# Linear attention with a norm, then an ELU MLP: the first batch worked in chunks of two heads

## The chip, the cores and the metric

The kernel runs on one core of a Trainium2 chip. Its engines work in parallel, each through its own list of instructions: PE (TensorE, matrix multiplies into PSUM, the accumulation memory), ACT (ScalarE, functions of one operand), DVE (VectorE, elementwise work), POOL (GpSimd, elementwise work, and here the issuer of most loads) and SP (SyncE, which issues other transfers). An engine takes its instructions strictly in order, so an instruction that waits holds up all behind it. Transfers between the chip's main memory and SBUF, the memory that the engines work on, are moved by 16 DMA engines that all queues share.

The metric is the device time of one execution in microseconds (us), as the median of several runs.

## The reference

```python
# q, k, v: (8, 8, 576, 64) float32; g_norm: (64,)
kv = np.einsum('bhsd,bhse->bhde', k, v)
out = np.einsum('bhsd,bhde->bhse', q, kv)
rms = np.sqrt(np.mean(out * out, axis=-1, keepdims=True) + 1e-06)
attn = out / rms * g_norm
# heads side by side: x is (8 * 576, 512)
x = attn.transpose(0, 2, 1, 3).reshape(B * S, H * D)
# w_in: (512, 2048), w_out: (2048, 512)
h = x @ w_in
g = np.where(h > 0.0, h, np.exp(np.minimum(h, 0.0)) - 1.0)
return g @ w_out
```

For each of 8 batches and 8 heads a 64x64 matrix K^T V is formed, Q is multiplied by it, and each row of 64 is divided by its root mean square and scaled by g_norm. The 4608 rows of 512 then go through two matrix multiplies with an ELU between them.

## The kernel before

**Tiles.** The 4608 rows of x are worked in nine tiles T of 512 rows. Matmuls take bf16 operands. For each tile the first multiply (mm1, line 378) makes h in eight pairs of 128x512 blocks, i = 0 to 7; each pair goes through the ELU (Exp on ACT, line 350; two operations on DVE, lines 358 and 362) into gT; the second multiply (mm2, line 399) takes gT in 16 blocks f against w_out, which arrives in four loads of four blocks each.

**Chunks.** A batch's q, k and v lie in SBUF as four chunks of two heads each, chunk m on 128 partitions with 9x64 columns. In the code a chunk has a number c = 2l + u. K^T V of a pair u = 0 (chunks 0 and 2) or u = 1 (chunks 1 and 3) is worked at once: `kv_mm` (line 152) issues 9 x 2 x 2 small matmuls. xT, the operand of mm1, has four parts c = 0 to 3, one for each chunk; mm1 needs all four to finish a block.

**The steps of a pair in tile 0**, which is batch 0 but for its last 64 rows of 576: q is turned by PE (`turned_q`, line 502) and copied to qT (`q_t_out`); K^T V is formed in PSUM and copied to kv_sb (`kv_out`, one half on DVE and one on ACT); the product y is made on PE (`y_mm`); then the class `Turned` squares y on ACT (line 229), PE takes the mean with a matrix of 1/64 (`mean_mm`, line 199), ACT makes Ln and Exp(-0.5 x) of it (`inv_t`, lines 208 and 209), and DVE multiplies y by that and by g (`scale_t`, line 212) into one part of xT.

**The head, in the order of the code** (lines 464 to 611). The order of all instructions on an engine is that of the code; it is written out by hand.

- SP loads batch 0 in fp32 by pairs of chunks: q, k, v of pair 0 (288 KB as bf16, 576 KB as fp32, each), then q and k of pair 1 and, into the buffer of the first q once this is cast, v of pair 1.
- DVE, ACT and, for pair 1, POOL cast these to bf16 (`first_cast`, columns low = 5 of 9 and high = 4 of 9).
- POOL issues all loads of the weights and of the later batches. These cast on the way from fp32 to bf16. Its list is: cast of q; w_in for blocks 0 to 4, rows 0 and 2; cast of k; the same, rows 1 and 3; cast of v; w_in for the other blocks in three loads; w_out(0); the first halves of q, k, v of batch 1; w_out(1); the second halves; w_out(2) and (3); batch 2; batch 3.
- PE fills its gaps with matmuls on zeros (`idle`, line 498): 9 at the start, then 10, 2, 1, 7 and 2, in all 31, into banks that are not in use.
- The first blocks of mm1 of tile 0 (`early`, line 578) are made part by part: h0, h1 and one half of h2 with parts c = 0 and 2, then c = 1, then c = 3, then the other half of h2 with all four. After these PE goes on with mm1 for i = 3 to 7 (line 611), and then with mm2 of tile 0 between the steps of batch 1 (lines 627 to 656).

PSUM has eight banks here under the tags A and B (pairs of banks), m and x (two single banks each). A new tile under a tag waits until the older one in the same bank has been read.

Of the kernel before, what the change touches and what calls it, by code (L numbers as in the profile page):

```python
# [16 lines left out]
def kernel(  # L17
# [90 lines left out]
    def copy_on(eng, out_, in_):  # L108
        if eng is nc.scalar:
            nc.scalar.copy(out_, in_)  # L110
# [40 lines left out]
    def kv_mm(b, kv_ps, u):
        for j in range(RK):
            for s in range(2):
                rows = slice(s * 64, s * 64 + 64)
                for l in range(2):
                    nc.tensor.matmul(  # L156
                        kv_ps[s][l * 64 : l * 64 + 64, u * 64 : u * 64 + 64],
                        lhsT=bf["k", b][rows, 2 * l + u, j, :],
                        rhs=bf["v", b][rows, 2 * l + u, j, :],
                        start=(j == 0),  # L160
                        stop=(j == RK - 1),
                    )
# [18 lines left out]
    def y_mm(T, u, ps, ns=slice(0, 8)):  # L181

        n = ns.start
        while n < ns.stop:
            b, j = slot_of(T, n)
            m = min(ns.stop - n, RK - j)
            for l in range(2):
                for s in range(2):
                    nc.tensor.matmul(  # L189
                        ps[l][s * 64 : s * 64 + 64, n * 64 : (n + m) * 64],  # L190
                        lhsT=kv_of(b, l, u, s),
                        rhs=qT[b][l * 64 : l * 64 + 64, s, u, j : j + m, :],
                        start=True,
                        stop=True,
                    )
            n += m

    def mean_mm(sq, ps):
        nc.tensor.matmul(ps, lhsT=ones, rhs=sq, start=True, stop=True)  # L199
# [7 lines left out]
    def inv_t(r, ps):  # L207
        nc.scalar.activation(r, ps, AF.Ln, bias=eps_col)  # L208
        nc.scalar.activation(r, r, AF.Exp, scale=-0.5)  # L209
# [251 lines left out]

    first = {}

    def first_load(name, u, st):
        first[name, u] = st
        load(st, name, 0, slice(u, 4, 2), nc.sync)

    def first_tile(name):  # L470
        return stage.tile([P, 2, RK, D], FP32, name=f"first_{name}", tag=f"first_{name}")

    def first_cast(name, u, eng, js):
        copy_on(eng, bf[name, 0][:, u::2, js, :], first[name, u][:, :, js, :])
# [14 lines left out]
    nc.vector.memset(zeros, 0.0)
    nc.vector.memset(eps_col, 1e-6)  # L490
    nc.vector.memset(one, 1.0)  # L491
    nc.vector.memset(ones, 0.0)
    for l in range(2):
        nc.vector.memset(ones[l * 64 : l * 64 + 64, l * 64 : l * 64 + 64], 1.0 / D)

    idle_ps = pair("B", "idle_ps")

    def idle(n, ps=idle_ps[:, 0, :]):
        for _ in range(n):
            nc.tensor.matmul(ps, lhsT=zeros[:, 0:P], rhs=zeros, start=True, stop=True)  # L500

    def turned_q(b, u, tag):

        ps = as_bf16(single(tag, "qt_ps"))
        q_t_mm(b, u, range(8), ps)
        return ps

    qT_tile(0)
    x_tile(0)
    g_ps = pair("A", "g_ps")  # L510
    idle(9)
    nc.tensor.transpose(g_ps[:, 0, 0:1], g_row.rearrange("o l e -> o (l e)"), one)
    nc.vector.tensor_copy(out=g_col, in_=g_ps[:, 0, 0:1])
    first_cast("q", 0, V, low)
    first_cast("q", 0, A, high)
    first_load("v", 1, first_tile("q"))
    ps = turned_q(0, 0, "m")
    idle(10)
    q_t_out(0, 0, V, ps, slice(0, 8))
    first_cast("k", 0, A, high)  # L520
    first_cast("k", 0, V, low)
    first_cast("v", 0, V, low)
    first_cast("v", 0, A, high)
    kv_ps = [single("x", "kv_ps") for _ in range(2)]
    kv_mm(0, kv_ps, 0)
    idle(2)
    kv_out(0, kv_ps, 0, (V, A))
    first_cast("q", 1, V, low)
    first_cast("q", 1, Q, high)
    load_w_in(slice(0, 5), slice(0, KC, 2))  # L530
    first_cast("k", 1, Q, high)
    load_w_in(slice(0, 5), slice(1, KC, 2))
    first_cast("v", 1, Q, high)
# [16 lines left out]
    y_ps = pair("A", "y_ps")  # L550
    n0.product([y_ps[:, l, :] for l in range(2)])
    for l in range(2):
        n0.square(l)
    ps = turned_q(0, 1, "m")
    q_t_out(0, 1, V, ps, slice(0, 8))
    first_cast("k", 1, V, low)
    first_cast("v", 1, V, low)
    idle(1)
    for l in range(2):
        n0.sums(l, single("x", "mean"))  # L560
        n0.inv(l)
    idle(7)
    kv_ps = pair("B", "kv_ps")
    kv_ps = [kv_ps[:, s, :] for s in range(2)]
    kv_mm(0, kv_ps, 1)
    kv_out(0, kv_ps, 1, (V, A))
    n0.scale(0)
    n0.scale(1)
    y_ps = [single("m", "y_ps") for _ in range(2)]
    idle(2, y_ps[0])  # L570
    n1.product(y_ps)
    for l in range(2):
        n1.square(l)
    g_tile(0)
    h0, h1 = pair("B", "h_ps"), pair("A", "h_ps")
    mean, h2 = single("x", "mean"), [single("x", "h_ps"), None]

    def early(h, i, a, cs):

        for c in cs:  # L580
            nc.tensor.matmul(  # L581
                h[a] if isinstance(h, list) else h[:, a, :],
                lhsT=w_in_sb[:, c, (2 * i + a) * P : (2 * i + a) * P + P],
                rhs=xT[0][:, c, :],
                start=(c == 0),
                stop=(c == KC - 1),
            )

    for a in range(2):
        early(h0, 0, a, (0,))  # L590
    n1.sums(0, mean)
    n1.inv(0)
    n1.scale(0)
    for a in range(2):
        early(h0, 0, a, (2,))
    for a in range(2):
        early(h1, 1, a, (0, 2))
    n1.sums(1, mean)
    n1.inv(1)
    n1.scale(1)  # L600
    early(h2, 2, 0, (0, 2))
# [181 lines left out]
```

## Time and profile before

| | |
|---|---|
| median of 7 runs | 294.97 us (294.12 to 295.32) |
| the profiled execution | 295.08 us |
| its span, first to last instruction | 293.3 us |
| mean granted TensorE clock in the span | 0.997 |
| first square of batch 0 on ACT | 10.19 us after the span's start |
| first matmul of `early` | 16.37 us |
| first matmul of mm1 for i = 3 | 22.86 us |
| POOL's first load (w_in) issued | 10.64 us |
| w_out(2) wanted by PE until | 42.47 us |

In the timeline each line holds the start, the duration, the engine, the line of the code, the operation, what it writes and reads, the shapes, the count of instructions merged into it and, in brackets, how long the engine sat idle before it and what ended that. In the table of stages each engine has its busy time and, in brackets, its count; then come the granted clock, the busy share of the DMA engines and what they moved in GB/s. A matmul of 128x512 is listed with 379 ns of busy time, but they overlap: eight start within 1.73 us, so one each 0.216 us.

### The profile page before, as it was taken

Reading aid. Unit: us, or ns where it says so; the run is one execution under the profiler, and the core shown is the slowest. Engines: PE = TensorE matmul, PEld = TensorE weight load, DVE = VectorE, ACT = ScalarE, POOL = GpSimd, SP = SyncE. Lnnn points to the kernel's source line nnn. Section 1 sums busy time; section 2 is a strip of 40 time slices with the busy share of each in tenths; the row PEclk is TensorE's granted clock in tenths of the full one; section 3 lists DMA queues with packets and bytes.
Section 4 is the critical chain, followed back from the end, with each engine's and each line's share of the span. In section 5 each row is a group of like instructions: output and inputs, shape, how many; then the busy total and the mean of one; then the engine's idle time right before and its main releaser. Section 6 shows DMA issues by size and latency. Waiting matters only on the chain.

```text
span 293.3 us, 5198 instructions
## 1 busy us (share of the span) xinstructions
PE 282.5 (96%) x2152; PEld 130.1 (44%) x2152; DVE 167.2 (57%) x221; ACT 142.1 (48%) x210; POOL 44.8 (15%) x79
## 2 busy tenths in 40 slices
PE   7979989998999999999999999999999999999994
PEld 3434434443444444444444444444444444444443
DVE  2538823478259855874577557755775677444600
ACT  3658445768555525542554255425542554244310
POOL 0663432213300002403300330000000000000000
PEclk9999999999999999999999999999999999999998
DMA  7999999996921089968943896362331214020222
GB/s 261 269 171 206 208 204 208 310 233 192 187 43 36 18 132 247 213 88 182 252 112 70 162 260 131 63 128 72 38 82 26 72 37 105 2 74 0 72 72 75
DMA packets 46236, 38.95 MB, mean 133 GB/s; under 512 B 26372, under 2 KB 38916, under 8 KB 46212
## 3 DMA queue, kind: packets, MB, share of 16 engines
q0 software_dynamic: 14144, 19.53, 34.2%
q1 hardware_dynamic: 31664, 18.55, 28.7%
q10 hardware_dynamic: 404, 0.53, 0.5%
q8 instruction: 17, 0.28, 0.4%
q14 instruction: 7, 0.06, 0.1%
HBM read 36.70 MB, written 9.44 MB: 157 GB/s over the span
## 4 chain that ended last, share of the span: by engine, by line
PE 79%; DMA 12%; DVE 3%; POOL 2%; ACT 2%; SPq 0%; issue 0%; DVEq 0%
PE o_ps L399 38%; PE h_ps L378 37%; DMA w_out_sb<-in_moe_w_out_dram 9%; DMA st_q<-in_q_dram 3%; DVE gT L362 2%; PE at L250 2%; POOL w_in_sb L116 1%; PE at L156 1%; PE o_ps L436 1%; ACT elu_e L350 1%; DVE elu_e L358 1%; DVE xT L212 0%; SPq L90 0%; PE qt_ps L174 0%; POOL q_bf L112 0%
## 5 line engine op out<-in xcount | busy, mean ns | idle before, releaser
L399 PE MATMUL o_ps<-w_out_sb,gT 128*128 128x512 bf16 x560 | 130.9, 379 | 1.5 <-DMA w_out_sb<-in_moe_w_out_dram 0.8
L378 PE MATMUL h_ps<-xT,w_in_sb 128*128 128x512 bf16 x552 | 128.9, 379 | 0.9 <-DVE gT L362 0.6
L350 ACT ACTIVATE elu_e<-h_ps 128x1024 bf16<-128x1024 f32 (+1 forms) x77 | 73.9, 972 | 92.1 <-PE h_ps L378 89.2
L362 DVE TENSOR_TENSOR gT<-elu_e,h_ps 128x1024 bf16<-128x1024 bf16 (+1 forms) x73 | 85.6, 1177 | 7.3
L399 PEld LDWEIGHTS <-gT 128*128 128x128 bf16 x560 | 54.4, 98 | 67.7 <-issue 3.3
L378 PEld LDWEIGHTS <-w_in_sb 128*128 128x128 bf16 x552 | 52.4, 98 | 62.6 <-issue 2.0
L358 DVE TENSOR_SCALAR elu_e<-elu_e 128x1024 bf16<-128x1024 bf16 x72 | 31.8, 441 | 68.4 <-ACT elu_e L350 68.2
L415 ACT COPY o_sb<-o_ps 128x512 f32<-128x512 f32 x32 | 18.5, 588 | 18.8 <-PE o_ps L399 18.7
L103 POOL CAST q_bf<-st_q 128x384 bf16<-128x384 f32 x30 | 14.2, 523 | 28.0 <-DMA st_q<-in_q_dram 28.0
L212 DVE SCALAR_TENSOR_TENSOR xT<-y_ps,g_col,rT 128x512 bf16<-128x512 f32 x12 | 8.9, 748 | 16.0 <-ACT rT L209 16.0
L283 DVE TENSOR_REDUCE ss<-sq 128x16 f32<-128x1024 bf16 x12 | 14.6, 1219 | 4.6 <-ACT sq L277 4.6
L299 DVE TENSOR_TENSOR xs<-at,ss 128x1024 bf16<-128x1024 f32 x12 | 14.6, 1217 | 0.0
L277 ACT ACTIVATE sq<-at 128x1024 bf16<-128x1024 f32 x12 | 12.3, 1028 | 1.0 <-PE at L250 1.0
L339 POOL COPY gate<-qT 1x32 bf16<-1x32 bf16 x4 | 0.8, 201 | 73.6 <-DMA qT<-q_bf 73.6
L229 ACT ACTIVATE sq<-y_ps 128x512 bf16<-128x512 f32 x12 | 6.5, 595 | 7.7 <-PE y_ps L189 7.7
L500 PE MATMUL idle_ps<-zeros 128*128 128x512 bf16 x29 | 9.0, 456 | 1.2 <-DVE one L491 1.2
L208 ACT ACTIVATE rT<-mean,eps_col 128x512 f32<-128x512 f32 x12 | 8.2, 683 | 3.0 <-PE mean L199 2.8
L156 PEld LDWEIGHTS <-k_bf 64*64 64x64 bf16 x576 | 5.7, 107 | 5.1 <-issue 4.2
L581 PE MATMUL h_ps<-xT,w_in_sb 128*128 128x512 bf16 x24 | 6.0, 379 | 1.9 <-DMA w_in_sb<-in_moe_w_in_dram 1.3
L209 ACT ACTIVATE rT<-rT 128x512 f32<-128x512 f32 x12 | 7.6, 630 | 0.4
L90 POOL DMA_DIRECT2D k_bf<-in_k_dram x9 | 6.6, 738 | 5.3 <-DMA w_in_sb<-in_moe_w_in_dram 1.9
L90 POOL DMA_DIRECT2D v_bf<-in_v_dram x9 | 6.8, 752 | 4.3 <-DMA w_out_sb<-in_moe_w_out_dram 1.8
(59 smaller groups left out, 97.5 us busy)
## 6 DMA issues: line engine op xcount, KB each, us to landing
out_dram<-o_sb SPq DMA_DIRECT2D x24, 256.0 KB, 4.1
st_q<-in_q_dram POOLq DMA_DIRECT2D x5, 1152.0 KB, 7.4
k_bf<-in_k_dram POOLq DMA_DIRECT2D x5, 576.0 KB, 9.4
v_bf<-in_v_dram POOLq DMA_DIRECT2D x5, 576.0 KB, 13.5
out_dram<-o_sb SPq DMA_DIRECT2D x19, 128.0 KB, 2.6
w_out_sb<-in_moe_w_out_dram POOLq DMA_DIRECT2D x4, 512.0 KB, 13.9
q_bf<-in_q_dram POOLq DMA_DIRECT2D x4, 288.0 KB, 14.0
k_bf<-in_k_dram POOLq DMA_DIRECT2D x4, 288.0 KB, 14.2
```

What stands on the lines that cost most here:

```text
L90: eng.dma_start(out=dst.rearrange("p m j d -> p m (j d)"), in_=in_[:, ms, :])
L103: nc.gpsimd.tensor_copy(out=bf["q", b][:, u, js], in_=raw[b][:, u::2, js, :].rearrange("p l j d -> p j l d"),)
L277: nc.scalar.activation(sq, st["se", h], AF.Square)
L283: nc.vector.reduce_sum(out=ss, in_=st.pop(("sq", h)).rearrange("p l (m e) -> p (l m) e", e=D), axis=AX.X,)
L299: nc.vector.tensor_tensor(out=st["xs"][:, 2 * h : 2 * h + 2, :].rearrange("p i (l m e) -> p l i m e", l=2, e=D), in0=se_ps.rearrange("p l ...
L350: nc.scalar.activation(e[:, lo:hi, :], h, AF.Exp)
L358: nc.vector.tensor_scalar(out=e, in0=e, scalar1=1.0, scalar2=1.0, op0=ALU.min, op1=ALU.subtract)
L362: nc.vector.tensor_tensor(out=gT[T][:, 2 * i + lo : 2 * i + hi, :], in0=e[:, lo:hi, :], in1=h, op=ALU.add if relu else ALU.max,)
L378: nc.tensor.matmul((ps[a] if isinstance(ps, list) else ps[:, a, :])[:, cols], lhsT=w_in_sb[:, c, f * P : f * P + P], rhs=xT[T][:, c, cols] ...
L399: nc.tensor.matmul(o_ps[T, j], lhsT=gT[T][:, f, j * P : j * P + P], rhs=w_out_sb[:, f, :], start=(f == 0), stop=(f == FC - 1),)
L415: nc.scalar.copy(o_sb[T, half][:, j % 2, :], o_ps[T, j])
L500: nc.tensor.matmul(ps, lhsT=zeros[:, 0:P], rhs=zeros, start=True, stop=True)
```

## The change

Tile 0's part of batch 0 is worked chunk by chunk, in the order 0, 2, 1, 3, where it was worked in two pairs.

- **Loads.** SP loads three pieces in fp32: q of chunks 0 and 2, k of chunk 0, v of chunk 0. All other pieces of batch 0 are loads on POOL's queue that cast on the way, straight into the bf16 tiles. POOL's list is: k and v of chunk 2; q of chunks 1 and 3; k and v of chunk 1; w_in for blocks 0 to 4, row 0; k and v of chunk 3; the same blocks of w_in, rows 2, 1, 3, in a load each; and from there the loads of before in their order. POOL's casts of batch 0 go, and DVE's and ACT's casts of pair 1.
- **K^T V.** `kv_mm` and `y_mm` take the halves l to work on as an argument. Each chunk has 18 matmuls and one copy of 64x128 on DVE in place of 36 matmuls and two copies of 128x64 for a pair.
- **Norm.** Square, mean, Ln, Exp and scale are issued for each chunk by itself. For chunks 1 and 3 Exp and scale are in two halves of 256 columns (`chunk_norm`). ACT's order is: square, Ln, Exp of chunk 0; of chunk 2; square, Ln, two Exps of chunk 1; of chunk 3. DVE's order is: copies of K^T V of chunks 0 and 2, the copy of qT of pair 1, scale 0, K^T V of chunk 1, scale 2, both halves of scale 1, K^T V of chunk 3, both halves of scale 3.
- **PE.** 13 matmuls on zeros (8 and 5) where there were 31, all before K^T V of chunk 0. The `early` matmuls are spread between the steps of chunks 1 and 3, and taken part by part in the order 0, 2, 1, 3.

The core of the diff:

```diff
-    def kv_mm(b, kv_ps, u):
+    def kv_mm(b, kv_ps, u, ls=range(2)):
...
-                for l in range(2):
+                for l in ls:
...
     for name in "qkv":
         bf[name, 0] = qkvp.tile([P, 4, RK, D], BF16, name=f"{name}_bf", tag=name)
-        first_load(name, 0, first_tile(name))
-    more = stage.tile([P, 4, RK, D], FP32, name="st_q", tag="q")
-    for name, half in (("q", 0), ("k", 2)):
-        first_load(name, 1, more[:, half : half + 2])
+    first = {"q": first_load("q", (0, 2)), "k": first_load("k", (0,)), "v": first_load("v", (0,))}
...
+    def chunk_load(name, cs):
+        ms = slice(cs[0], cs[-1] + 1, 2)
+        load(bf[name, 0][:, ms], name, 0, ms)
+    chunk_load("k", (2,))
+    chunk_load("v", (2,))
+    chunk_load("q", (1, 3))
+    chunk_load("k", (1,))
+    chunk_load("v", (1,))
+    load_w_in(slice(0, 5), slice(0, 1))
+    chunk_load("k", (3,))
+    chunk_load("v", (3,))
+    for c in (2, 1, 3):
+        load_w_in(slice(0, 5), slice(c, c + 1))
...
+    def chunk_kv(kv_ps, c):
+        kv_mm(0, [kv_ps[:, s, :] for s in range(2)], c % 2, (c // 2,))
+    def chunk_kv_out(kv_ps, c, eng):
+        rows, cols = slice(c // 2 * 64, c // 2 * 64 + 64), slice(c % 2 * 64, c % 2 * 64 + 64)
+        copy_on(eng, kv_sb[rows, 0, c % 2], kv_ps[rows, :, cols])
+    def chunk_y(c, tag):
+        y_ps[c] = single(tag, "y_ps")
+        y_mm(0, c % 2, {c // 2: y_ps[c]}, (c // 2,))
+    def chunk_square(c):
+        sq0[c] = attp.tile([P, G], BF16, name="sq", tag="sq")
+        nc.scalar.activation(sq0[c], y_ps[c], AF.Square)
+    def chunk_inv(c, mean):
+        r0[c] = outp.tile([P, G], FP32, name="rT", tag="o")
+        inv_t(r0[c], mean)
+    def chunk_scale(c):
+        scale_t(0, y_ps[c], r0[c], c)
+    def chunk_norm(c, mean):
+        r0[c] = outp.tile([P, G], FP32, name="rT", tag="o")
+        nc.scalar.activation(r0[c], mean, AF.Ln, bias=eps_col)
+        for n in range(2):
+            cols = slice(n * 256, n * 256 + 256)
+            nc.scalar.activation(r0[c][:, cols], r0[c][:, cols], AF.Exp, scale=-0.5)
+            scale_t(0, y_ps[c][:, cols], r0[c][:, cols], c, cols)
...
+    idle(8, kv_ps[:, 0, :])
+    first_cast("q", (0, 2), V, low)
+    first_cast("q", (0, 2), A, high)
+    ps = turned_q(0, 0, "m")
+    idle(5, kv_ps[:, 0, :])
+    q_t_out(0, 0, V, ps, slice(0, 8))
...
+    chunk_kv(kv_ps, 0)
+    chunk_kv_out(kv_ps, 0, V)
+    chunk_y(0, "x")
+    chunk_square(0)
+    chunk_kv(kv_ps, 2)
+    chunk_kv_out(kv_ps, 2, V)
+    mean = pair("A", "mean")
+    mean_mm(sq0[0], mean[:, 0, :])
+    chunk_inv(0, mean[:, 0, :])
+    chunk_y(2, "x")
+    chunk_square(2)
+    ps = turned_q(0, 1, "m")
+    q_t_out(0, 1, V, ps, slice(0, 8))
+    mean_mm(sq0[2], mean[:, 1, :])
+    chunk_inv(2, mean[:, 1, :])
+    chunk_scale(0)
+    kv_ps = pair("B", "kv_ps")
+    chunk_kv(kv_ps, 1)
+    chunk_kv_out(kv_ps, 1, V)
+    chunk_scale(2)
+    chunk_y(1, "m")
+    chunk_square(1)
...
+    early(h0, 0, 0, (0,))
+    early(h0, 0, 1, (0,))
+    mean_mm(sq0[1], mean)
+    chunk_norm(1, mean)
+    early(h2, 2, 0, (0,))
+    chunk_kv(kv_ps, 3)
+    chunk_kv_out(kv_ps, 3, V)
+    chunk_y(3, "m")
+    chunk_square(3)
+    early(h1, 1, 0, (0,))
+    early(h1, 1, 1, (0,))
+    early(h0, 0, 0, (2,))
+    mean_mm(sq0[3], mean)
+    chunk_norm(3, mean)
...
```

More of the change, by code (lines that the diff above doesn't have):

```diff
@@ L179, in q_t_out, with y_mm @@
         copy_on(eng, qT[b][:, :, u, js, :], src.rearrange("p (j s r) -> p s j r", s=2, r=64))
-    def y_mm(T, u, ps, ns=slice(0, 8)):
-        n = ns.start
-        while n < ns.stop:
+    def y_mm(T, u, ps, ls=range(2)):
+        n = 0
+        while n < 8:
             b, j = slot_of(T, n)
-            m = min(ns.stop - n, RK - j)
-            for l in range(2):
+            m = min(8 - n, RK - j)
+            for l in ls:
                 for s in range(2):
@@ L460, in store, with first_load @@
                 nc.sync.dma_start(out=rows[b1][:, j1, :], in_=o[hs, 1, :])
[L464 to L474, printed above, removed]
+    def first_load(name, cs):
+        st = stage.tile([P, len(cs), RK, D], FP32, name=f"first_{name}", tag=f"first_{name}")
+        load(st, name, 0, slice(cs[0], cs[-1] + 1, 2), nc.sync)
+        return st
     low, high = slice(0, 5), slice(5, 9)
@@ L487 @@
     make_identity(nc, ident)
[L489 to L533, printed above, removed]
+    def chunk_load(name, cs):
[11 more added lines that the diff above has]
+        load_w_in(slice(0, 5), slice(c, c + 1))
     for lo, hi in ((5, 9), (9, 13), (13, 16)):
@@ L548 @@
     cast_q(3)
-    n0, n1 = Turned(0, 0), Turned(0, 1)
-    y_ps = pair("A", "y_ps")
-    n0.product([y_ps[:, l, :] for l in range(2)])
+    nc.vector.memset(zeros, 0.0)
+    nc.vector.memset(eps_col, 1e-6)
+    nc.vector.memset(one, 1.0)
+    nc.vector.memset(ones, 0.0)
     for l in range(2):
[L553 to L576, printed above, removed]
+        nc.vector.memset(ones[l * 64 : l * 64 + 64, l * 64 : l * 64 + 64], 1.0 / D)
@@ new lines, in idle, with turned_q, first_cast @@
+    def idle(n, ps):
+        for _ in range(n):
+            nc.tensor.matmul(ps, lhsT=zeros[:, 0:P], rhs=zeros, start=True, stop=True)
+    def turned_q(b, u, tag):
+        ps = as_bf16(single(tag, "qt_ps"))
+        q_t_mm(b, u, range(8), ps)
+        return ps
+    def first_cast(name, cs, eng, js):
+        copy_on(eng, bf[name, 0][:, cs[0] : cs[-1] + 1 : 2, js, :], first[name][:, :, js, :])
+    def chunk_kv(kv_ps, c):
+        kv_mm(0, [kv_ps[:, s, :] for s in range(2)], c % 2, (c // 2,))
@@ new lines, in chunk_kv_out @@
+    def chunk_kv_out(kv_ps, c, eng):
+        rows, cols = slice(c // 2 * 64, c // 2 * 64 + 64), slice(c % 2 * 64, c % 2 * 64 + 64)
+        copy_on(eng, kv_sb[rows, 0, c % 2], kv_ps[rows, :, cols])
+    y_ps, sq0, r0 = {}, {}, {}
+    def chunk_y(c, tag):
[7 more added lines that the diff above has]
+        inv_t(r0[c], mean)
@@ L587, in early @@
             )
[L589 to L601, printed above, removed]
+    qT_tile(0)
+    x_tile(0)
+    g_ps = pair("A", "g_ps")
+    kv_ps = pair("B", "kv_ps")
+    idle(8, kv_ps[:, 0, :])
+    nc.tensor.transpose(g_ps[:, 0, 0:1], g_row.rearrange("o l e -> o (l e)"), one)
+    nc.vector.tensor_copy(out=g_col, in_=g_ps[:, 0, 0:1])
+    first_cast("q", (0, 2), V, low)
[3 more added lines that the diff above has]
+    q_t_out(0, 0, V, ps, slice(0, 8))
+    first_cast("k", (0,), A, high)
+    first_cast("k", (0,), V, low)
+    first_cast("v", (0,), A, high)
+    first_cast("v", (0,), V, low)
+    chunk_kv(kv_ps, 0)
[14 more added lines that the diff above has]
+    chunk_scale(0)
+    kv_ps = pair("B", "kv_ps")
+    chunk_kv(kv_ps, 1)
[3 more added lines that the diff above has]
+    chunk_square(1)
+    g_tile(0)
+    h0, h2 = pair("A", "h_ps"), [None, None]
+    mean = single("x", "mean")
+    early(h0, 0, 0, (0,))
+    early(h0, 0, 1, (0,))
+    mean_mm(sq0[1], mean)
+    chunk_norm(1, mean)
+    h2[0] = single("x", "h_ps")
+    early(h2, 2, 0, (0,))
[3 more added lines that the diff above has]
+    chunk_square(3)
+    h1 = pair("B", "h_ps")
+    early(h1, 1, 0, (0,))
[3 more added lines that the diff above has]
+    chunk_norm(3, mean)
+    early(h0, 0, 1, (2,))
+    early(h1, 1, 0, (2,))
+    early(h1, 1, 1, (2,))
+    early(h2, 2, 0, (2,))
     for c in (1, 3):
@@ L607 @@
     h2[1] = single("x", "h_ps")
-    early(h2, 2, 1, (0, 2, 1, 3))
+    early(h2, 2, 1, range(KC))
     elu(0, 2, h2, True)()
```

## The prediction

> **What bounds the kernel now.** I read the page's busy shares first, then TensorE's waits, then the timeline of the first 45 us, engine by engine, and last the DMA rates stage by stage.
>
> ```profile
> PE 282.5 (96%) x2152; PEld 130.1 (44%) x2152; DVE 167.2 (57%) x221; ACT 142.1 (48%) x210; POOL 44.8 (15%) x79
> ```
>
> PE is the bound, so the change can only win what PE loses: idle time, and the 31 matmuls on zeros. After 45 us PE's waits are short ones for DVE (0.25 to 0.38 us), out of the change's reach. What it can reach lies before, and these lines of the timeline hold it:
>
> ```profile
> 8.23 0.62 ACT L110 CAST v_bf<-first_v 128x512 bf16<-128x512 f32 x1 [1.44 <-DMA first_v<-in_v_dram]
> 10.19 1.09 ACT L229 ACTIVATE sq<-y_ps 128x512 bf16<-128x512 f32 x2 [0.62 <-PE y_ps L189]
> ...
> 15.05 1.08 ACT L229 ACTIVATE sq<-y_ps 128x512 bf16<-128x512 f32 x2 [0.49 <-PE y_ps L189]
> 16.37 0.60 PE L581 MATMUL h_ps<-xT,w_in_sb 128*128 128x512 bf16 x2 [1.34 <-DMA w_in_sb<-in_moe_w_in_dram]
> 17.23 0.69 ACT L208 ACTIVATE rT<-mean,eps_col 128x512 f32<-128x512 f32 x1 [1.09 <-PE mean L199]
> 17.95 0.63 ACT L209 ACTIVATE rT<-rT 128x512 f32<-128x512 f32 x1
> 18.74 0.69 ACT L208 ACTIVATE rT<-mean,eps_col 128x512 f32<-128x512 f32 x1 [0.16 <-PE mean L199]
> 19.46 0.63 ACT L209 ACTIVATE rT<-rT 128x512 f32<-128x512 f32 x1
> 20.12 0.75 DVE L212 SCALAR_TENSOR_TENSOR xT<-y_ps,g_col,rT 128x512 bf16<-128x512 f32 x1 [0.76 <-ACT rT L209]
> 20.92 2.10 PE L581 MATMUL h_ps<-xT,w_in_sb 128*128 128x512 bf16 x9 [0.27 <-DVE xT L212]
> 22.86 8.80 PE L378 MATMUL h_ps<-xT,w_in_sb 128*128 128x512 bf16 x40
> ...
> 33.21 0.48 PE L156 MATMUL kv_ps<-v_bf,k_bf 64*64 64x64 bf16 x36 [0.36 <-DMA v_bf<-in_v_dram]
> 42.47 1.89 PE L399 MATMUL o_ps<-w_out_sb,gT 128*128 128x512 bf16 x8 [0.83 <-DMA w_out_sb<-in_moe_w_out_dram]
> ```
>
> The reader is to see three things. The head ends at 22.86, where mm1 of tile 0 runs on without a gap; it is set by a chain over ACT (square, Ln, Exp) and DVE (scale) whose last link, 20.92, needs the fourth chunk of xT. Inside that chain 1.3 us go to w_in, which lands at 16.3. And later PE waits twice more for a load, 0.36 at 33.2 and 0.83 at 42.5 (the third block of w_out).
>
> ```profile
> 3.00:5.00 2.00, 2.00 (x6) 0.47 (x4) 0.00 (x0) 0.33 (x1) 0.00 (x0) 1.00 1.04 409
> ...
> 11.50:13.00 1.50, 1.50 (x9) 0.67 (x7) 1.26 (x3) 1.28 (x3) 1.50 (x3) 1.00 0.26 37
> 13.00:15.00 2.00, 1.94 (x44) 0.87 (x42) 1.10 (x4) 1.45 (x4) 2.00 (x3) 1.00 1.08 172
> 15.00:16.50 1.50, 0.15 (x4) 0.11 (x2) 0.63 (x1) 1.08 (x2) 1.50 (x3) 1.00 1.09 142
> 16.50:18.00 1.50, 1.50 (x8) 0.69 (x7) 0.00 (x0) 0.74 (x2) 1.50 (x4) 1.00 0.88 124
> ...
> 24.00:30.00 6.00, 6.00 (x30) 2.70 (x29) 5.58 (x10) 5.00 (x9) 2.19 (x3) 1.00 1.24 206
> ```
>
> The last column is GB/s written. SP's fp32 loads run at about 400, GpSimd's casting loads at 206 (two bytes for every four read, so the same reading speed). Between them lies a hole: from 11.5 to 20 us the loads fall short of 206 by 1.5x169 + 2x34 + 1.5x64 + 1.5x82 + 2x6 = 550 KB, 2.7 us of transfer.
>
> **The change, part by part.**
>
> *1. GpSimd loads start at 1.3 us, not 10.64.* POOL's ident is done at 1.30, and then come 0.72 to 0.83 us for each issue. Eight loads go out by 7.2; each later one waits for the landing of the one eight before it, as now (w_out(1), tenth, leaves at 19.48 when the second w_in lands). POOL loses its three casts (0.93, 0.63, 0.93).
>
> *2. SP's three loads now share the engines.* They are 256+128+128 = 512 packets of 2304 B. Alone, 1373 such packets move in 8 us (172 per us); by 3.0 us 71 have moved (164 GB/s). GpSimd's first load needs 2.4 us from issue to speed (10.64 to 13.0), so sharing starts near 3.7, when SP has 191. How two queues share is shown where stores meet loads:
>
> ```profile
> q0 software_dynamic: 468, 0.52, 60.3%
> q1 hardware_dynamic: 471, 0.87, 52.6%
> ```
>
> That is 57 to 62 us: equal packets, some 90 per us each. The other 321 then take 3.6 us, to 7.3. Landing lags the last packet by 0.57 (q), 0.59 (k) and 1.15 us (v) now, so chunk 0 of v lands at 7.9 to 8.4; I take 8.2, which is where the pair of chunks lands today. Ends: no sharing, 3.0 + 441/172 + 0.6 = 6.15; even sharing from 3.0 on, 3.0 + 441/86 + 1.15 = 9.3.
>
> *3. From v to the first square.* Now 10.19 - 8.2 = 2.0 us. Half the cast (0.49 for 640 columns, 0.21 for a copy of 128: near 0.3) and 18 matmuls for 36 (0.48 busy, 0.2 of it latency: 0.14 less) leave 1.7. First square: 9.9.
>
> *4. Four serial rounds on ACT.* Now the squares of a pair run back to back, one round for two chunks. After, ACT's order is square, Ln, Exp for chunk 0, then 2, 1, 3, and each square waits behind the Exp before it. One round: square to mean 0.62 (0.595 and a handover), mean to Ln 0.42 (16.81 to 17.23), Ln to Exp 0.72 (17.23 to 17.95), Exp to the next on ACT 0.54 (12.40 to 12.94): 2.3 us. Square of chunk 1 at 9.9 + 4.6 = 14.5; its mean 15.1, Ln 15.55, halved Exps 16.25 and 16.6 (256 columns took 0.37 on ACT, 0.42 on DVE in the last column copies), second half of scale 17.05 to 17.5. On DVE the copy of chunk 3's K^T V is queued behind that half: 17.75. Product 17.9, square 18.35, mean 18.95, Ln 19.4, Exps 20.1 and 20.45, last half of scale 20.9 to 21.35. The c=3 matmuls start at 21.4 against 20.92: **0.5 us later**. The 9 other matmuls behind mean fit in between (9x0.216 from 19.2: 21.1), and after c=3 both kernels have the same 9, so mm1 follows at 23.35.
>
> *5. Waits of the chain on loads.* GpSimd's 1024 packets of batch 0 get 90 per us to 7.3 and 175 after: q of chunks 1 and 3 are in at 8.4, v of chunk 1 at 9.9, w_in row 0 (sixth load) near 10.6, v of chunk 3 at 12; with 1.5 us of lag 9.9, 11.4, 12.1, 13.5. They are needed at 11, 13.2, 14.1 and 15.5, so I cost them at nothing. The cover is 1.1 us at the least. v of chunk 2 is tighter: 128 packets for k, 128 for v, in by 6.5, landed at 8, wanted at 9.7; if it were 2 us later, mean 0 behind it on PE, and all rounds, would be 0.3 late.
>
> *6. The two later waits.* With no cold start at 11.5 the loads behind batch 0 come 1.2 us earlier (253 KB of the hole) if the 172, 142 and 124 belong to w_in itself, 2.7 if they belong to the start. PE wants the third block of w_out at 42.47 - 0.83 + 0.5 - 0.36 = 41.8 and gets it at 39.7 to 41.2; likewise at 33.2. Both waits go: **1.2 us saved**. They can save no more than that.
>
> *7. Fewer matmuls on zeros* (13 for 31, 0.216 or 0.427 each): nothing, since they fill idle time, unless the clock needs them; see the third rival. The new DVE copies of 64x128 (about 0.25 each) are in step 4.
>
> Sum: +0.5 - 1.2 = **-0.7 us**. The profiled execution took 295.08 (span 293.3, 1.8 around it), the median of 7 is 294.97, so 0.1 apart: 294.4 for such a profile, **294.3** as a median. The ends of step 2 make it -2.75 to +0.4, the handovers of step 4 add 0.5 either way.
>
> One rule speaks against step 1. The Trainium skill, "SBUF — State Buffer", section "SBUF: two separate sides", says that a VectorE copy of fp32 in SBUF locks GpSimd out of a shared port, so it cannot write descriptors and its loads starve. The rows: DVE's cast of k took 0.70 beside a POOL cast, not 0.49; but at 24 to 30 us, with DVE busy 5.58 of 6, the loads hold 206. By the rule the three early casts would push GpSimd's loads by about 1 us, an estimate from the cast rows, and the sum would stay inside step 5's cover; by the row they cost nothing.
>
> **Rivals.**
> *A. The loads don't share.* If GpSimd's first loads are slow to start, SP's finish at 6.15, the head ends 2 us earlier: -0.7 - 2.05 = -2.75, 292.2; half of it, 293.3. For: the first w_in load took 5.7 us to land. Against: 468 to 471 packets.
> *B. A wash.* v lands at 9, or step 5's chunk 2 is late, and the four rounds eat the 1.2: 294.6 to 295.5. For: 1.15 us of lag on v today. Against: nothing but the middle of my bounds.
> *C. Slower: the clock falls.* From 8.5 to 18 us PE would be busy about 4 of 9.7 us, with a gap of 2 us ahead of chunk 3's product. Matmuls on zeros took 0.427 until 5.2 us, where the granted clock rises to full; it fell 2.7 us after the last matmul at the end. If it falls at 12 to 18 us, small steps in the rounds cost some 0.8 and the next 4 us of matmuls go at half speed, 2.0: +2.8 - 0.7 = +2.1, 297.1. It decides from a granted clock of half in any stretch of 8 to 23. Against: the 1.34 us gap at 15.0 left it at 1.00. The Trainium skill, "TensorE: Matmul & The Clock Gate", section "Part 1: The HAM clock gate", has it fall after one idle window of about 3.4 us; a gap of 2 us would pass, and the sum would stand.
>
> **How the numbers follow.** Forecast 0.41 (own range 293.5 to 294.9), A 0.12, B 0.25, C 0.22. Two tenths of a per cent, 0.59 us, is what the measurement tells from no change. Faster: 0.31 of the forecast's and all of A, 0.43. Within: 0.10 of the forecast's, 0.13 of B, 0.01 of C, 0.24. Slower: 0.12 of B and 0.21 of C, 0.33. The range leaves out the better half of A and the worse third of C: 293.0 to 296.6.
>
> **What will show it.** SP's v lands near 8.2; first square near 9.9; squares 2.3 us apart, the fourth 3.8 behind the third; mm1 of i=3 at 23.35; no wait on a load at 33 or 42; GpSimd's rate at 206 from 8 us on; clock 1.00 from 5 or 9 us. I am wrong if v lands before 7.5 or after 8.8, if the clock dips, or if PE waits for q, k, v or w_in after 9 us.

## The result and the profile after

The changed kernel takes 298.52 us (median of 12 runs, 296.64 to 299.59) against 294.92 for the kernel before on the same chips: a ratio of 1.011, 95% interval 1.0094 to 1.0127. It is 3.6 us slower by the medians (3.2 by the ratio, which is taken over all executions) and outside the predicted range. The profiled execution took 298.65 with a span of 296.9, 3.6 more than before, so it can be read as a typical one. From its page, the span, the busy times and the granted TensorE clock in 40 slices of 7.4 us:

```profile
span 296.9 us, 5164 instructions
PE 284.3 (96%) x2134; PEld 130.7 (44%) x2134; DVE 165.9 (56%) x222; ACT 141.6 (48%) x210; POOL 47.4 (16%) x85
PEclk9959999999999999999999999999999999999999
```

The clock's row of the kernel before:

```profile
PEclk9999999999999999999999999999999999999998
```

One slice stands out: the third, 15 to 22 us, has 5 where before has 9. PE has 18 matmuls less to run and is still busy 1.8 us longer. The next table has the changed kernel's head in stretches of 3.41 us, which is the step of the clock's own records. The records change 0.12 us ahead of these cuts, so a 0.98 or 0.52 below is 1.00 or 0.50 by the clock's own step (busy us of PE, PEld, DVE, ACT and POOL, each with its count; then the granted clock, the share of the DMA engines, GB/s):

```profile
6.72:10.13 3.41, 3.02 (x30) 1.23 (x29) 1.45 (x4) 0.41 (x1) 1.65 (x4) 1.00 1.21 205
10.13:13.54 3.41, 1.98 (x40) 1.16 (x37) 1.40 (x3) 2.40 (x4) 2.63 (x4) 0.98 1.15 168
13.54:16.95 3.41, 3.03 (x25) 1.12 (x24) 1.27 (x3) 1.91 (x3) 3.12 (x5) 0.50 1.21 206
16.95:20.37 3.42, 2.00 (x23) 0.82 (x22) 1.17 (x3) 1.61 (x4) 0.72 (x2) 0.50 1.24 206
20.37:23.78 3.41, 3.41 (x10) 1.18 (x9) 0.63 (x2) 1.80 (x4) 0.71 (x1) 0.52 1.28 205
```

From 13.42 to 23.66 us the clock is at half. It fell at the end of a stretch in which PE is listed busy for 1.98 of 3.41 us, and came back only after one in which PE had no gap. (The trace's clock records begin at 10.00; before that matmuls on zeros started 0.427 us apart, so the 1.00 in the first row is a default and the clock first rose at 10.00. In the kernel before it rose at 4.96.) The timeline of PE and ACT in the changed kernel (start, duration, line, count; in brackets the idle time ahead and what ended it):

```profile
6.70 2.31 PE L519 MATMUL kv_ps<-zeros 128*128 128x512 bf16 x5
...
8.95 0.69 PE L156 MATMUL kv_ps<-v_bf,k_bf 64*64 64x64 bf16 x18
...
10.46 0.60 ACT L545 ACTIVATE sq<-y_ps 128x512 bf16<-128x512 f32 x1 [3.00 <-PE y_ps L189]
...
12.78 0.58 ACT L545 ACTIVATE sq<-y_ps 128x512 bf16<-128x512 f32 x1
...
15.67 0.60 ACT L545 ACTIVATE sq<-y_ps 128x512 bf16<-128x512 f32 x1 [0.29 <-PE y_ps L189]
...
20.17 0.60 ACT L545 ACTIVATE sq<-y_ps 128x512 bf16<-128x512 f32 x1 [1.66 <-PE y_ps L189]
...
21.74 5.00 PE L566 MATMUL h_ps<-xT,w_in_sb 128*128 128x512 bf16 x18
...
26.58 1.89 PE L378 MATMUL h_ps<-xT,w_in_sb 128*128 128x512 bf16 x8
...
29.79 0.38 PE L378 MATMUL h_ps<-xT,w_in_sb 128*128 128x512 bf16 x1 [1.32 <-DVE gT L362]
```

The reader sees the four squares, 2.3, 2.9 and 4.5 us apart, eighteen `early` matmuls spread over 5.0 us of which the first part runs at half clock, mm1 of i=3 at 26.58 instead of 22.86, and behind it a wait that before did not have: block i=4 has to wait 1.32 us for DVE. The waits of before on v of batch 1 (0.36) and on w_out (0.83) are gone, and one of 0.17 for DVE:

```profile
32.25 0.59 PE L399 MATMUL o_ps<-w_out_sb,gT 128*128 128x512 bf16 x2 [0.17 <-DVE gT L362]
```

The account: 3.72 + 1.32 - 0.36 - 0.83 - 0.17 = 3.7, against 3.6 in the spans.

### The profile page after: what moved, and what is told of

Read it like the earlier page. It is cut to its first block, busy times and chain, and to the rows that moved or that the text cites. A ratio compares the mean times of both kernels' runs of the same rounds, so it can differ in the third digit from the quotient of the medians.

```text
span 296.9 us, 5164 instructions
## 1 busy us (share of the span) xinstructions
PE 284.3 (96%) x2134; PEld 130.7 (44%) x2134; DVE 165.9 (56%) x222; ACT 141.6 (48%) x210; POOL 47.4 (16%) x85
## 4 chain that ended last, share of the span: by engine, by line
PE 91%; DVE 4%; ACT 3%; DMA 1%; issue 0%; DVEq 0%
PE o_ps L399 40%; PE h_ps L378 40%; PE h_ps L566 2%; PE kv_ps L519 2%; DVE gT L362 2%; PE at L250 2%; PE qt_ps L174 1%; PE at L156 1%; PE mean L199 1%; ACT elu_e L350 1%; PE y_ps L189 1%; PE kv_ps L156 1%; PE o_ps L436 1%; DMA out_dram<-o_sb 1%; DVE elu_e L358 1%; DVE xT L212 1%
## 5 line engine op out<-in xcount | busy, mean ns | idle before, releaser
L378 PE MATMUL h_ps<-xT,w_in_sb 128*128 128x512 bf16 x552 | 128.9, 379 | 2.1 <-DVE gT L362 1.9
L358 DVE TENSOR_SCALAR elu_e<-elu_e 128x1024 bf16<-128x1024 bf16 x72 | 31.1, 432 | 70.2 <-ACT elu_e L350 69.9
L212 DVE SCALAR_TENSOR_TENSOR xT<-y_ps,g_col,rT 128x512 bf16<-128x512 f32 (+1 forms) x14 | 9.2, 671 | 18.5 <-ACT rT L209 12.8
L156 PEld LDWEIGHTS <-k_bf 64*64 64x64 bf16 x576 | 7.0, 111 | 7.1 <-issue 7.0
L90 POOL DMA_DIRECT2D k_bf<-in_k_dram x12 | 8.8, 730 | 5.5 <-PE y_ps L189 2.1
L90 POOL DMA_DIRECT2D v_bf<-in_v_dram x12 | 8.3, 694 | 4.8 <-DMA w_out_sb<-in_moe_w_out_dram 1.7
L208 ACT ACTIVATE rT<-mean,eps_col 128x512 f32<-128x512 f32 x10 | 6.8, 683 | 2.9 <-PE mean L199 2.7
L566 PE MATMUL h_ps<-xT,w_in_sb 128*128 128x512 bf16 x24 | 8.1, 487 | 0.0
L229 ACT ACTIVATE sq<-y_ps 128x512 bf16<-128x512 f32 x8 | 4.3, 596 | 6.4 <-PE y_ps L189 6.4
L519 PE MATMUL kv_ps<-zeros 128*128 128x512 bf16 x13 | 5.9, 630 | 1.2 <-DVE one L512 1.2
L312 DVE TENSOR_SCALAR xT<-xT,g_col 128x1024 bf16<-128x1024 bf16 x12 | 5.8, 480 | 2.2 <-DMA xT<-xs 2.2
```

Source lines behind the costliest of these rows:

```text
L156: nc.tensor.matmul(kv_ps[s][l * 64 : l * 64 + 64, u * 64 : u * 64 + 64], lhsT=bf["k", b][rows, 2 * l + u, j, :], rhs=bf["v", b][rows, 2 * ...
L358: nc.vector.tensor_scalar(out=e, in0=e, scalar1=1.0, scalar2=1.0, op0=ALU.min, op1=ALU.subtract)
L378: nc.tensor.matmul((ps[a] if isinstance(ps, list) else ps[:, a, :])[:, cols], lhsT=w_in_sb[:, c, f * P : f * P + P], rhs=xT[T][:, c, cols] ...
L566: nc.tensor.matmul(h[a] if isinstance(h, list) else h[:, a, :], lhsT=w_in_sb[:, c, (2 * i + a) * P : (2 * i + a) * P + P], rhs=xT[0][:, c, :],
```

## The experiments

Two suspects follow from that account, and both are edits of a few lines: the clock, and the pair of PSUM banks that block i=4 waits for. A third is the order of DVE, and a last question is what the loads gave. All times are medians; each ratio is to the kernel before, run on the same chip, and is taken over all executions, so it can differ from that of the two medians.

| run | us | before | ratio (95% interval) |
|---|---|---|---|
| e1 zeros in the gaps | 295.60 | 294.80 | 1.0037 (1.0019 to 1.0055) |
| e2 banks exchanged | 297.31 | 294.80 | 1.0078 (1.0053 to 1.0104) |
| e3 both | 294.35 | 294.80 | 0.9996 (0.9977 to 1.0014) |
| e4 before, with 13 zeros | 295.54 | 294.80 | 1.0020 (1.0005 to 1.0035) |
| e5 e3, copy of chunk 3 first | 292.41 | 295.11 | 0.9908 (0.9890 to 0.9926) |
| e6 e3, chunks 1 and 3 as a pair | 292.70 | 295.11 | 0.9917 (0.9894 to 0.9941) |
| e7 e6, 2 zeros for 5 | 292.68 | 295.11 | 0.9914 (0.9896 to 0.9932) |
| e8 before, loads alone | 293.77 | 295.11 | 0.9959 (0.9938 to 0.9981) |
| e9 orders of e5, no added zeros | 294.92 | 294.89 | 1.0003 (0.9983 to 1.0024) |
| e10 e5, one zero less at the start | 292.66 | 294.89 | 0.9948 (0.9926 to 0.9969) |
| e11 e5, nine zeros less | 293.35 | 294.89 | 0.9957 (0.9940 to 0.9974) |

### e1: matmuls on zeros in PE's gaps

```diff
+    def fill(n, c, tag):
+        if c not in y_ps:
+            y_ps[c] = single(tag, "y_ps")
+        idle(n, y_ps[c])
...
     def chunk_y(c, tag):
-        y_ps[c] = single(tag, "y_ps")
+        fill(0, c, tag)
...
     nc.vector.tensor_copy(out=g_col, in_=g_ps[:, 0, 0:1])
+    idle(1, kv_ps[:, 0, :])
...
     chunk_kv(kv_ps, 0)
+    fill(2, 0, "x")
...
+    fill(1, 2, "x")
     mean_mm(sq0[0], mean[:, 0, :])
...
+    fill(5, 1, "m")
     mean_mm(sq0[2], mean[:, 1, :])
...
     chunk_kv(kv_ps, 1)
+    fill(2, 1, "m")
...
+    fill(2, 3, "m")
     mean_mm(sq0[1], mean)
...
     chunk_kv(kv_ps, 3)
+    fill(7, 3, "m")
```

> The changed kernel with 20 more matmuls on zeros in PE's gaps between 5 and 20 us (one behind g's transpose, then 2, 1, 5, 2, 2 and 7 into the bank of the next product), nothing else changed. Theory 1 (the granted clock fell to half because PE was too little busy): clock 1.00 from some 5 to 8 us on, mm1 of i=3 near 23.4 instead of 26.6, time 295.3, about 3.2 us below the changed kernel and 0.1% above before. Rival (the four serial rounds on ACT and DVE cost it, whatever the clock): 298 or more, and mm1 still later than 25.5. If clock and rounds share it: between 296 and 297.5.

Measured: 295.60 against the 295.3 of theory 1 and the 298 of the rival. The granted clock rises at 3.99 us and stays at 1.00. The timeline of this run, the five zeros ahead of the first K^T V, the four squares on ACT, DVE's two halves of scale 1 with the copy of K^T V of chunk 3 behind them, and PE's mm1:

```profile
6.15 1.25 PE L519 MATMUL kv_ps<-zeros 128*128 128x512 bf16 x5
...
9.14 0.60 ACT L550 ACTIVATE sq<-y_ps 128x512 bf16<-128x512 f32 x1 [1.36 <-PE y_ps L189]
11.45 0.58 ACT L550 ACTIVATE sq<-y_ps 128x512 bf16<-128x512 f32 x1
13.78 0.60 ACT L550 ACTIVATE sq<-y_ps 128x512 bf16<-128x512 f32 x1
...
16.12 0.87 DVE L212 SCALAR_TENSOR_TENSOR xT<-y_ps,g_col,rT 128x256 bf16<-128x256 f32 x2 [1.49 <-ACT rT L565]
17.03 0.29 DVE L112 CAST kv_sb<-kv_ps 64x128 bf16<-64x128 f32 x1
...
17.82 0.60 ACT L550 ACTIVATE sq<-y_ps 128x512 bf16<-128x512 f32 x1 [1.43 <-PE y_ps L189]
...
20.98 2.10 PE L571 MATMUL h_ps<-xT,w_in_sb 128*128 128x512 bf16 x8 [0.19 <-DVE xT L212]
...
22.92 1.89 PE L378 MATMUL h_ps<-xT,w_in_sb 128*128 128x512 bf16 x8
...
26.29 7.07 PE L378 MATMUL h_ps<-xT,w_in_sb 128*128 128x512 bf16 x32 [1.48 <-DVE gT L362]
```

With 20 more matmuls that compute nothing, mm1 of i=3 starts at 22.92, where before has 22.86. The 3.7 us by which the head was late were the clock: its late first rise and its fall, which this execution has neither of (e3 tells the two apart). The squares stand 2.31, 2.33 and 4.04 us apart, and the wait for the banks is still there, 1.48.

### e2 and e3: the banks

```diff
-    for i, tag in zip(range(3, 8), "mBAxm"):
+    for i, tag in zip(range(3, 8), "mABxm"):
         mm1(0, i, tag, tag == "x")()
...
-    for tag, j0 in (("A", 0), ("B", 2)):
+    for tag, j0 in (("B", 0), ("A", 2)):
```

> The changed kernel with mm1's block 4 in the PSUM pair A and block 5 in B (after: B, then A), and mm2's four sums likewise exchanged. In the changed kernel PE waits 1.3 us at 28.5 for DVE to finish block 1 of the ELU, since h1 lies in B there. Theory 2 (the exchanged pairs cost those 1.3 us whatever the clock does): that wait goes, 297.2. Rival (the wait hides work that PE would wait for anyway, for example at the first mm2 or at the loads): 298.2 or more, with a wait of about 1 us elsewhere before 60 us.

> Both edits of the two runs before. Theories 1 and 2 add up: 295.3 - 1.3 = 294.0, 0.3% below before. If the clock alone matters: 295.3. If neither does: 298.5. If the saved waits on loads (1.2 us) come back: 295.2.

Before, h0 lay in the pair B and h1 in A, and mm1's blocks i=4 and 5 took B, then A. The change put h0 into A and h1 into B and left mm1's order, so block 4 asks for the pair that the ELU frees second. With the exchange PE runs 35 matmuls of e2 in one piece (line of PE's timeline):

```profile
26.37 7.93 PE L378 MATMUL h_ps<-xT,w_in_sb 128*128 128x512 bf16 x35
```

e2 gives 297.31 (theory 297.2), e3 294.35 (theory 294.0). Against the kernel before the changed kernel is +3.6, zeros alone make it +0.8, banks alone +2.5, both -0.45: 2.8 and 1.1 apart, 4.05 together (by the means of all executions 2.3 and 1.0, and 3.4). The two causes add up and, within the noise, explain the whole loss.

The profiled execution of e3 shows what the clock's share is made of. Its clock rose only at 10.04 us, as in the changed kernel, and then stayed up:

```profile
6.91 2.31 PE L519 MATMUL kv_ps<-zeros 128*128 128x512 bf16 x5
...
24.65 8.80 PE L378 MATMUL h_ps<-xT,w_in_sb 128*128 128x512 bf16 x40
```

mm1 starts at 26.58 with a late rise and a fall (the changed kernel), at 24.65 with a late rise alone (e3) and at 22.92 with neither (e1): the fall is worth some 1.9 us there, the late rise 1.7. The zeros of e1 and e3 did away with the fall; the late rise comes and goes between executions. e1's times lie in two groups, seven from 294.98 to 295.72 and five from 296.56 to 296.86, and e3's too, eight from 293.73 to 294.39 and four from 295.67 to 296.06. e1's profiled execution (295.49) is from the lower group, e3's (295.74) from the upper. That the early or late rise makes the groups fits both profiles; the other executions have no trace to show it. Of the kernel before, too, only one execution has a trace, with a rise at 4.96, so whether the change made late rises more frequent is open.

### e4: the kernel before with the changed kernel's zeros

```diff
-    idle(9)
+    idle(8)
...
-    idle(10)
+    idle(5)
...
     kv_mm(0, kv_ps, 0)
-    idle(2)
...
-    idle(1)
...
-    idle(7)
...
-    idle(2, y_ps[0])
```

> The kernel before with 13 matmuls on zeros, 8 and 5, all ahead of the first K^T V, as in the changed kernel, and none of the later 12; nothing else changed. Theory 1: the clock falls to half somewhere between 8 and 25 us here too, and it takes 1.5 to 3.5 us more than before (296.4 to 298.4). Rival (the matmuls on zeros are not needed, the changed order of work is to blame): 294.9 within 0.4, clock 1.00 throughout.

Measured: 295.54, 0.7 above before. The direction is theory 1's, the size is below its range. Two stages of this run, in the columns used above:

```profile
9.99:13.40 3.41, 1.85 (x22) 0.79 (x23) 2.20 (x4) 2.82 (x5) 3.41 (x5) 0.97 0.69 204
13.40:16.81 3.41, 2.85 (x43) 1.44 (x44) 1.54 (x3) 2.08 (x5) 3.41 (x6) 0.50 0.97 124
```

The clock falls here too, from 13.22 to 20.05 us (0.18 us ahead of the cuts), after a stretch with PE listed busy for 1.85 of 3.41. mm1 of i=3 comes at 24.06, 1.2 late. But before has waits for loads in this part: those for w_in (1.34) and for v of batch 1 (0.36) are gone here, as PE comes later, and half of the lateness never reaches the end. Zeros are worth less where a load sets the pace anyway; the changed kernel has no such wait to hide behind.

### e5: the copy of chunk 3's K^T V first

```diff
+    chunk_kv(kv_ps, 3)
+    chunk_kv_out(kv_ps, 3, V)
     fill(2, 3, "m")
     mean_mm(sq0[1], mean)
     chunk_norm(1, mean)
...
-    chunk_kv(kv_ps, 3)
-    fill(7, 3, "m")
-    chunk_kv_out(kv_ps, 3, V)
     chunk_y(3, "m")
```

> The kernel of e3 (zeros in the gaps, banks exchanged) with K^T V of chunk 3 and its copy on DVE issued ahead of chunk 1's mean, so that the copy no longer queues behind both halves of scale 1. Theory 3 (the fourth round is late because of that queue: in e1 square 4 starts 4.04 us after square 3, the other rounds are 2.3): square 4 comes 2.6 us after square 3, mm1 of i=3 1.4 us earlier than in e3 for the same clock, 293.0. Rival (PE's own matmuls, or a load, or the later waits take the place): 293.9 to 294.4.

The edit is against e3; the seven zeros go with the gap that they filled. Measured: 292.41, 2.7 below before, better than expected. In the profile (ACT's fourth square, PE's mm1):

```profile
16.62 0.58 ACT L550 ACTIVATE sq<-y_ps 128x512 bf16<-128x512 f32 x1
...
21.70 8.80 PE L378 MATMUL h_ps<-xT,w_in_sb 128*128 128x512 bf16 x40
```

The fourth square comes 3.03 us after the third (13.59), not 4.04, and mm1 1.2 us before that of e1, whose clock rose as early. The expectation had 2.6 and 1.4. The median gained 2.2 on e3, each against its own runs of before. A part of that is e3's upper group: e5's six executions lie from 292.40 to 293.00, and the profiled one saw its clock rise at 5.03. Whether the edit keeps the late rise away, or six executions were too few to meet it, is open.

### e6 and e7: the last two chunks as a pair

```diff
     kv_ps = pair("B", "kv_ps")
-    chunk_kv(kv_ps, 1)
-    chunk_kv_out(kv_ps, 1, V)
+    for c in (1, 3):
+        chunk_kv(kv_ps, c)
+        chunk_kv_out(kv_ps, c, V)
     chunk_scale(2)
+    fill(1, 1, "m")
+    for c in (1, 3):
+        chunk_y(c, "m")
+        chunk_square(c)
...
+    for c in (1, 3):
+        mean = single("x", "mean")
+        mean_mm(sq0[c], mean)
+        chunk_norm(c, mean)
```

The later fills and the `early` matmuls between the chunks go or follow in one piece. e7 also has `idle(2)` for `idle(5)` ahead of the first K^T V.

> The kernel of e3 with chunks 1 and 3 worked as a pair, as both pairs were before: both K^T V, both products, both squares back to back, then mean, Ln, Exps and scale of 1 and of 3; chunks 0 and 2 stay as in the change. Theory 4 (the serial rounds on ACT are a cost of their own, 2.3 us each instead of 1.3 in a pair): mm1 of i=3 2.3 to 2.7 us earlier than in e3 for the same clock; the wait for the third block of w_out, 40.0 in the changed kernel, comes back with 0.3 to 0.8; 292.3 to 292.9. Rival (v of chunk 3 lands too late to be worked so early): PE waits for it between 12 and 15 us, and 293.5 or more.

> The kernel of e6 with 2 instead of 5 matmuls on zeros behind the first transposes. In e3 these ran at half clock until 9.1 us, while K and V of chunk 0 were cast at 8.2. If that delay costs in most executions: 0.5 us below e6 (291.8 to 292.5). If fewer zeros let the clock rise a window later, or fall again: 0.5 to 1.5 above e6.

Measured: 292.70 and 292.68. Theory 4's time is met, but not by its path. PE's waits in e6:

```profile
13.68 0.47 PE L156 MATMUL kv_ps<-v_bf,k_bf 64*64 64x64 bf16 x18 [0.70 <-DMA v_bf<-in_v_dram]
...
40.01 1.89 PE L399 MATMUL o_ps<-w_out_sb,gT 128*128 128x512 bf16 x8 [0.29 <-DMA w_out_sb<-in_moe_w_out_dram]
```

mm1 comes at 21.27, 1.65 before e1's and not 2.3 to 2.7, since PE now waits 0.70 for v of chunk 3 (the rival's sign), and 0.29 of what is left goes to w_out again. Loads hold this version up again, and e5, which works chunk by chunk to the end, is as fast. Fewer zeros (e7) changed nothing that can be told.

### e8: the loads alone

```diff
-    more = stage.tile([P, 4, RK, D], FP32, name="st_q", tag="q")
-    for name, half in (("q", 0), ("k", 2)):
-        first_load(name, 1, more[:, half : half + 2])
...
-    first_load("v", 1, first_tile("q"))
...
-    first_cast("q", 1, V, low)
-    first_cast("q", 1, Q, high)
+    for name in "qkv":
+        load(bf[name, 0][:, 1::2], name, 0, slice(1, 4, 2))
     load_w_in(slice(0, 5), slice(0, KC, 2))
-    first_cast("k", 1, Q, high)
     load_w_in(slice(0, 5), slice(1, KC, 2))
-    first_cast("v", 1, Q, high)
```

The two casts of k and v on DVE further down go as well.

> The kernel before with the loads of the second pair moved to GpSimd's queue, casting on the way, ahead of all weights; their six casts on DVE and POOL go; order of work, pairs and zeros as before. It is the load part of the change alone. Theory: sharing delays the first pair's v from 8.2 to 9 or 10, w_in lands some 2 us earlier, the waits for w_in (1.3), v of batch 1 (0.36) and w_out (0.83) go: 293.6 to 294.4. Rival (the early loads cost the first pair more than they give): 295.0 or more, with the first square after 12. Second rival (the clock falls in the wider gap ahead of the first pair): 295.5 or more and a granted clock of half after 8 us.

Measured: 293.77, 1.3 below before, inside the theory's range. From the timeline, the zeros and the first K^T V on PE with ACT's cast of the first pair's v between them, and PE's mm1:

```profile
6.10 2.33 PE L497 MATMUL idle_ps<-zeros 128*128 128x512 bf16 x10
...
9.46 0.62 ACT L110 CAST v_bf<-first_v 128x512 bf16<-128x512 f32 x1 [2.77 <-DMA first_v<-in_v_dram]
...
10.01 0.48 PE L156 MATMUL kv_ps<-v_bf,k_bf 64*64 64x64 bf16 x36 [1.58 <-DVE v_bf L112]
...
22.69 8.81 PE L378 MATMUL h_ps<-xT,w_in_sb 128*128 128x512 bf16 x39
```

v lands 1.2 us later than before, as said, yet mm1 is 0.2 earlier, and PE has no wait on a load from the `early` matmuls to 60 us. Moving the loads is a gain, then, in the old order of work too. The second rival's condition was there, a gap of 1.58 us on PE, and the clock stayed at 1.00: in this run's step of the clock from 7.25 to 10.66 us PE is listed busy for only 1.68 us, less than in any step behind which it fell in the head of other runs (1.91 at the least). The step holds four or five of the 128x512 matmuls on zeros.

### e9, e10, e11: which zeros are needed

e9 is the changed kernel with the edits of e2 and e5 and without the added zeros; e10 and e11 are e5 less these:

```diff
 # e10
-    idle(1, kv_ps[:, 0, :])
 # e11
-    fill(5, 1, "m")
...
-    fill(2, 1, "m")
...
-    fill(2, 3, "m")
```

> The changed kernel with both orders mended (banks exchanged, copy of chunk 3's K^T V ahead of the norm of chunk 1) and its own 13 matmuls on zeros. If the clock is a cost of its own beside the orders: the clock still falls at 10 to 14 us, 295.5 to 296.5, that is 3 to 4 us above e5. Rival (with the tighter order PE is busy enough and the clock stays up): within 0.6 us of e5's 292.4. Second rival (the copy's queue mattered only because the clock was low): 297.3 as in e2.

> The kernel of e5 without the one matmul on zeros behind g's transpose; the 12 between the steps of the chunks stay. Theory (the time goes with the second stretch of half clock, from 10 or 14 to 24 us, not with the moment of the first rise): 292.4 within 0.4, though the clock may rise only near 10 us in some executions. Rival (the late first rise costs most of it): 294 or more.

> The kernel of e5 without the zeros of 11 to 15 us (5, 2 and 2): PE then runs only its own small work between the mean of chunk 0 and the c=0 matmuls, with no gap over 1.3 us. In the changed kernel and in e4 the clock fell after a stretch of 3.4 us in which PE is listed busy for 1.85 to 1.98 us. Theory (a stretch of low share is enough, no long gap is needed): the clock falls at 12 to 16 us in most executions, 293.5 to 295.5. Rival (only the two-microsecond gap ahead of chunk 3's product did it, and this is gone): 292.4 within 0.4, clock 1.00.

e9: 294.92, slightly below its range, and no different from before. The clock falls in every one of its executions (means of 0.983 to 0.993 over the span); in the profiled one after the first of these two stages:

```profile
8.75:12.17 3.42, 1.99 (x41) 1.07 (x38) 1.65 (x3) 2.40 (x4) 2.03 (x3) 0.98 1.12 163
12.17:15.58 3.41, 3.03 (x41) 1.41 (x42) 1.21 (x3) 1.92 (x3) 3.00 (x5) 0.50 1.20 206
```

Both orders mended thus win back just the loss, and the zeros are worth 2.5 us on top by the medians, 2.8 by the ratios (e5). e10: 292.66, as the theory said, but by its median only. Seven executions took 292.15 to 292.73, the profiled one with a first rise at 4.62; five took 293.91 to 294.84, near the rival's 294, and e5 has none there. So a cost of the late rise is likely, as in e3, and that the one zero at the start does not matter is not shown. e11: 293.35, between the two answers. The mean clock was 0.993 in two of seven executions and 0.997 or more in the others. That the clock falls without the long gap ahead of chunk 3's product is shown by e9 (in the changed kernel, too, it had fallen before that gap); that these nine zeros alone decide it is not.

## Why the prediction was wrong, step by step

**Step 7 failed: the matmuls on zeros were costed at nothing.** The prediction named the condition ("unless the clock needs them"), made it rival C, priced it at 2.8 us and gave it 0.22. e1 measures 2.8 between medians, 2.3 between means. The rival's mechanism was right, a fall at 12 to 18 us (it came at 13.42); its chance was not. Its price was met in part by luck: the fall costs 1.9 at mm1, and the late first rise, for which the rival had no term, adds 1.7 in the profiled execution. The chance was judged by the longest gap on PE, from a gap of 1.34 us that had left the clock up and from the rule in the Trainium skill ("TensorE: Matmul & The Clock Gate", section "Part 1: The HAM clock gate") that an idle window of some 3.4 us lowers the clock. In the changed kernel it fell after 3.41 us in which the longest gap was 1.02 us and PE was listed busy for 1.98. That rule and this trace differ, and the trace decides: it fell without an idle window. The prediction had a warning in hand ("about 4 of 9.7 us"; from 8.5 to 18 it is 9.5 us, and the trace lists 7.3 of them, part at half clock) and did not use it. What the clock does go by is open: e8 kept it with a longer gap, 1.58 us, and a smaller listed share, 1.68 of 3.41.

**Step 4 failed at its end.** "After c=3 both kernels have the same 9, so mm1 follows" stopped the account at mm1's first block. The pairs of PSUM banks of h0 and h1 had changed places, which stands in the diff, and block i=4 took the one that comes free last: 1.3 us in the profile, 1.1 to 1.3 between medians (e2 against the change, e3 against e1). The prediction had no term and no rival for it. It is what moved the time from rival C's 297.1 to 298.5.

**Steps 1 and 2 held but for a size.** POOL's first load was issued at 1.45, the eighth by 6.3. v of chunk 0 landed at 7.05, not 8.2, and outside the prediction's own 7.5 to 8.8: GpSimd's packets set in only at about 4.7, 3.2 us after the issue where the step took 2.4 from the w_in load. From there the two queues did share evenly. Their packets from 5 to 6 us in the changed kernel (packets, MB, share of the engines):

```profile
q0 software_dynamic: 87, 0.10, 57.7%
q1 hardware_dynamic: 84, 0.19, 54.4%
```

DVE's early casts held GpSimd's loads up in no way that the trace shows: from 7 to 8 us, with DVE casting K and V from 7.42 to 7.99, GpSimd's queue alone wrote 206 GB/s.

**Step 3** gave 1.7 from v to the first square. It took 3.4, since PE stood at five zeros at half clock (6.70 to 8.95) while K and V were cast by 8.0; in e1, at full clock, 1.8. This is the late first rise, and no term of the sum allowed for it.

**Step 4's rounds held.** 2.3 us each was measured as 2.31 and 2.33 (e1), and the fourth square 3.85 later as 4.04, for the reason given: DVE's copy behind both halves of scale 1. e5 shows that reason by removing it: 3.03. By luck in two sizes, the head of e1 ends near the 23.35 of the sum, at 22.92: v came 0.8 early (7.37), and the rest took 0.4 longer.

**Steps 5 and 6 held.** In the changed kernel PE never waits for q, k, v or w_in from 8 us on, though the loads fell short of 206 GB/s for a while (144 from 10 to 12 us), and both later waits are gone; e8 shows that the loads alone win 1.3 us. In e3, where banks and the fall of the clock are mended, the time is 0.45 below before by the medians, where the forecast had 0.7; the ratio, 0.9996 (0.9977 to 1.0014), does not tell it from no change.

## What to carry to other kernels

Work that computes nothing has a price when it goes: before such matmuls are removed, don't look at the longest gap alone. Where the new order leaves PE some 3.4 us of small matmuls with a listed share of about 0.55 to 0.65, keep the clock's half rate as a term of the sum with a chance that counts, and try the order with and without zeros; e8 and e11 show that the share alone does not decide. Compare executions, not one profile, as the first rise moves between them. When a change hands out PSUM banks in another order, follow each bank to its next user and see which is read out last. The fastest version here, e5 (e6 and e7 can't be told from it), keeps the change's loads and chunks, and adds 13 matmuls on zeros and two edits of order: 0.9908 of before (0.9890 to 0.9926).

## What the runs showed of the hardware

- The granted clock changed only at steps of 3.41 us: it stayed at half for 10.24 (three such steps) in the changed kernel and in e2, and for 6.83 (two) in e4 and e9. Counted over the clock's own steps, it fell behind 1.97 us of listed PE work of 3.41 in the changed kernel, 1.91 in e4, 1.99 in e9 and 2.23 in e2; steps of 2.19 (e11), 2.14 (e7) and 1.68 (e8) passed. The listed time is thus no measure of what the clock goes by. In the four steps behind which it fell, one or two matmuls are listed as 128*128 128x512, beside transposes (128*64) and products of 64*64; in the three that passed, three or more. That the smaller matmuls count for less would fit this; no run tests it by itself.
- The clock first rose at 3.99, 5.03 and 10.04 us in e1, e5 and e3, which start alike. Continuous zeros from 1.19 to 4.6 us were enough in some executions and not in others, so the moment of the first rise can't be read from one profile.
- A load that casts, issued first on an idle GpSimd at 1.45 us, moved its first packets near 4.7; from 5 to 6 us its queue and SP's moved 87 and 84 packets.
